# Two halves of P times V summed in PSUM by VectorE, the memory's part added per group of heads, and lead units in other banks, in a kernel of four interleaved blocks

## The chip, the cores and the metric

The kernel runs on one core of a Trainium2 chip. The metric is the time of one execution on the device, in microseconds (us). A core has one engine for matmuls (PE, TensorE) with its queue of weight loads (PEld), and three others: DVE (VectorE), ACT (ScalarE) and POOL (GpSimd). SP (SyncE) issues the transfers (DMA) used here. Each engine works through its own instructions in a fixed order, so an instruction that waits holds up all that stand behind it on that engine. PE writes to PSUM, which has eight banks of 128 partitions by 512 float32; all else lies in SBUF. A name such as L1412 is line 1412 of the kernel's file. In the changed kernel the numbers are 1 to 11 higher: L1412 is L1421 there, L1426 is L1437.

## The reference

The input x is 1 x 2048 x 640, the result has the same shape. Two blocks, A and B, take turns, each with a LayerNorm ahead and the input added behind:

```
x = x + A(layernorm(x));  x = x + B(layernorm(x))      # twice

A: q, k, v = x @ wq, x @ wk, x @ wv     # 32 heads of 20, 4 segments of 512
   for each segment s:
       a_dot = softmax(q k^T * scale + mask) v          # within the segment
       a_mem = (phi(q) M) / (phi(q) z + 1e-6)           # phi(t) = t + 1 if t > 0 else exp(t)
       o     = sigmoid(beta) * a_mem + (1 - sigmoid(beta)) * a_dot
       M, z  = M + phi(k)^T v, z + sum(phi(k))
   return o @ wo
B: z = gelu(x @ w_in)                   # 640 -> 1728
   z1, z2 = z[:864], layernorm(z[864:])
   return (z1 * (w_sp @ z2 + b_sp)) @ w_out
```

The mask takes out the keys that lie *before* the query in a segment, and keeps the query's own and those behind it. M and z are zero in the first segment, so no memory is read there.

## The kernel before

**Number format.** Every large matmul is done with fp16 operands: a number is split into a high half (its fp16 value) and a low half (what is left, again in fp16), and of the four products three are summed. Splits are the bulk of the work beside PE: for the probabilities P, ACT takes the exponential (L1358) and the high half (L1376), POOL the low half (L1377).

**Stages, as they lie in the profiled execution.** Up to 113 us: loads, the scaling of weights, and the lead of the first attention layer. 113 to 612 us: first attention. 612 to 1221 us: first mixer (block B: its first phase ends with `zp`, L334; the second multiplies along the tokens, L713, and goes back with `cyp`, evicted at L749). From 1207, partly inside the mixer's end, to 1254: lead of the second attention layer. 1254 to 1736: second attention. 1736 to 2271: second mixer.

**Attention.** Heads go in pairs; two pairs take NS = 5 steps (so there are two combines in five steps, 64 of each kind in the two layers), and a step t of the program consists, on PE, of

- the scores for the row maxima `mp` of step t + 8 (LM = 8), with keys as columns, and the scores `es` of step t with keys as rows, each with its mask matmuls (L1351, L1322). DVE reduces `mp` to maxima (L1365, L1368), ACT takes exp of `es`;
- every five steps, the transpose of the maxima `mtp` (L1384), which go back as a bias row of the queries by way of the split at L1387 and DMAs (L1390);
- matmuls that fill the time: the projection to queries and keys (`unit`, L1185), to values (L1128) and the output projection (`yps`, L1161), drawn from generators along the string `order` ("02 03 v4 04 v5 ..."); the memory's `update` (L1277) and `read` (L1247) at fixed steps, with `post` for what follows one or more steps later;
- P times V, `pvs` (L1412), of step t - 2 (LV = 2). Its left operands are P's halves, its right ones V of a head as 41 columns: 20 of V's high half, one of ones (the row sum of P), 20 of V's low half. So one matmul gives the product with both halves of V side by side, 41 columns per head and 128 queries, and a pair of heads fills 8 x 41 = 328 columns of one bank.

After the third and the fifth of five steps a pair is complete, and `combine` (L1417) follows: DVE forms 1 / (row sum * gate) in `rs` (L1425, L1426), multiplies all 328 columns by it into the SBUF tile `ab` (L1430), and POOL adds the two halves into `oat` (L1431) and, from the second segment on, the memory's part `gm` (L1433). After the last pair of a group (6 heads, the fifth group 8) the inner function `out` runs two steps later: ACT copies `oat` to fp16 (L1441), POOL subtracts (L1442), SP stores (L1447).

**PE's order** is written out by hand: the attention phases and the mixer's first phase stand under a manual schedule for PE, so PE's rows are in program order. **The order on DVE, ACT, POOL and SP** is set by a scheduler that plays the program through with costs of its own; it may put any instruction ahead of another that it doesn't depend on. A tile of a pool that is laid on addresses of an earlier tile waits for that tile's last reader, wherever the tile was named. So a change of the size of one tile shifts others, and with them what waits for what.

**PSUM.** The pool of tag `dn` has banks 0 and 1 (projections), `mp` 2 and 3, `ms` 4 (transposes, updates, reads), `es` 5 and 6, `pv` 7. There is one buffer for each tag but `dn`, which has two.

**The lead.** Before step 0 there are LEAD = 12 steps, -12 to -1, in which projections of the first segment run before any probability is there; `mp` starts at step -8. The units of head rows (0,0) and (0,1) (segment, row of 128) are done ahead of the lead, and their two memory updates are kept in `self.wait` until the lead; (0,2) and (0,3), v4 and (0,4) come in the lead itself. Each k goes from its bank through `out`: scaled high and low halves, then exp and max for phi, which is written back to the bank, and `keys` reads it from there (L1218, L1219).

**The mixer's first phase** loads x1 rows (L293), makes their statistics and LayerNorm (L235 to L244) and splits (L250, L252), and multiplies (`zp`, L334).

## Time and profile before

| | |
|---|---|
| three runs | 2265.99, 2270.63, 2275.52 us; median 2270.63 us |
| profiled execution | 2273.17 us; span from first to last instruction 2271.4 us |
| granted PE clock, mean over the span | 0.985 |
| PE busy | 2121.0 us, 93% |
| PEld busy (overlaps PE) | 1292.5 us, 57% |
| DVE | 1467.5 us, 65% |
| ACT | 1167.1 us, 51% |
| POOL | 991.0 us, 44% |
| transfers | 349 MB, mean 154 GB/s |

The profile is of one execution. Its rows come in a few forms. A stretch reads `from:to length`, then for PE, PEld, DVE, ACT and POOL the busy time with the count of instructions in brackets, then the granted clock of PE (1.00 is full), the share of time in which the transfer engines were busy, and GB/s. A row of waits reads: who waited, the line, for which instruction of which engine, us in total, how often, the longest. A row of the timeline reads: start, duration, engine, line, operation, destination and sources with shapes, how many of the same were joined in the row, and in brackets how long the engine had stood before it and what ended that. A row of a group reads the same without a start: count, then busy us and mean ns of one, then idle time just before and its releasers. Shares of the span are means over stages of different kinds: POOL's 44% holds the mixer's second phases, in which it does almost nothing.

### The profile page before, as it was taken

To read this page: it belongs to the slowest core of one execution; us is meant where nothing else is said; L and a number is where in the kernel's file an instruction comes from. 1 tells how busy PE (TensorE), PEld (TensorE's weight loads), DVE (VectorE), ACT (ScalarE), POOL (GpSimd) and SP (SyncE) were. 2 spreads that over 40 slices of the span, in tenths; PEclk is the share of its full clock that TensorE was granted. 3 is DMA by queue.
4 is the path that set the end of the run, shared out by engine and by line. 5 is a ranking of instruction groups with operands and counts; after the bars stand their busy time and mean duration, and the time that the engine had idled before them with its cause. 6 is when DMAs were issued, how large, how long until landed. Compare 5 with 4: busy or idle time off the path is not lost. (4 is left out here: it accounts for less than half of the span.)

```text
span 2271.4 us, 49058 instructions
## 1 busy us (share of the span) xinstructions
PE 2121.0 (93%) x19911; PEld 1292.5 (57%) x19911; DVE 1467.5 (65%) x2686; ACT 1167.1 (51%) x1400; POOL 991.0 (44%) x804
## 2 busy tenths in 40 slices
PE   4888898988699999999998898999999999999999
PEld 2455565656455555555554556666665555555655
DVE  8588878686744555545433787786766767455455
ACT  3298888786622332222222797888875334323221
POOL 2198989987610100100001698889985323000000
PEclk9999999998999999999999999999999999999999
DMA  5534634455645669977756345344467334977876
GB/s 163 152 107 112 175 96 128 117 148 138 160 122 153 169 174 230 239 224 190 177 150 153 84 101 149 88 116 109 125 179 182 94 109 104 257 211 190 226 209 135
DMA packets 511428, 349.02 MB, mean 154 GB/s; under 512 B 409889, under 2 KB 447649, under 8 KB 506081
## 3 DMA queue, kind: packets, MB, share of 16 engines
q1 hardware_dynamic: 511200, 345.88, 58.7%
q8 instruction: 156, 2.56, 0.5%
q14 instruction: 72, 0.58, 0.1%
HBM read 156.51 MB, written 101.21 MB: 113 GB/s over the span
## 5 line engine op out<-in xcount | busy, mean ns | idle before, releaser
L1377 POOL TENSOR_TENSOR PHL<-P,PHL 128x1024 f16<-128x1024 f32 x310 | 659.0, 2134 | 155.3 <-ACT PHL L1376 149.1
L1358 ACT ACTIVATE P<-es,sc 128x1024 f32<-128x1024 f32 x320 | 355.9, 1112 | 109.6 <-PE es L1322 101.0
L1368 DVE TENSOR_REDUCE mx<-mp 128x2 f32<-128x1024 f32 (+2 forms) x384 | 319.8, 859 | 51.4 <-PE mp L1322 51.1
L238 POOL TENSOR_TENSOR lnrs<-lnve,mhalf 128x1 f32<-128x1 f32 x92 | 56.4, 621 | 656.5 <-DVE lnve L237 627.7
L1376 ACT CAST PHL<-P 128x1024 f16<-128x1024 f32 x320 | 333.3, 1042 | 5.8
L334 PEld LDWEIGHTS <-th 128*128 128x128 f16 x1920 | 188.2, 98 | 179.0 <-DMA th<-xnhl 16.1
L713 PE MATMUL gp<-zh,wt 128*128 128x432 f16 x1024 | 231.2, 346 | 0.0
L713 PEld LDWEIGHTS <-wt 128*128 128x128 f16 x1536 | 150.2, 98 | 128.9
L1412 PEld LDWEIGHTS <-PHL 128*128 128x128 f16 x5120 | 166.5, 96 | 73.6 <-DVE ab L1430 22.0
L499 PEld LDWEIGHTS <-wt 128*128 128x128 f16 x1344 | 131.3, 98 | 113.4 <-DMA wt<-wn 1.1
L1412 PE MATMUL pv<-vs,PHL 128*128 128x41 f16 x5120 | 174.2, 181 | 22.3 <-DVE ab L1430 14.1
L1128 PE MATMUL vps<-wvh,xt 128*128 128x320 f16 x640 | 155.3, 305 | 15.4 <-DVE vs L1134 12.7
L334 PE MATMUL zp<-wi1h,th 128*128 128x432 f16 x640 | 150.0, 349 | 14.9 <-DMA th<-xnhl 14.6
L1351 PE MATMUL mp<-qk 60*128 60x512 f16 (+3 forms) x1024 | 126.6, 305 | 23.5 <-DVE mx L1368 14.1
L1351 PEld LDWEIGHTS <-qk 60*128 60x128 f16 (+1 forms) x2048 | 78.8, 94 | 116.2 <-issue 94.8
L1351 PE MATMUL es<-qk 64*128 64x256 f16 (+3 forms) x1024 | 124.5, 298 | 17.2 <-ACT P L1358 9.2
L713 PE MATMUL gp<-zl,wt 128*128 128x432 f16 x512 | 135.3, 346 | 0.0
L1185 PE MATMUL kps<-xt,wkh 128*128 128x512 f16 x380 | 124.5, 390 | 8.1 <-DVE phl L1219 8.1
L1185 PE MATMUL qps<-xt,wqh 128*128 128x512 f16 x380 | 122.1, 383 | 0.9 <-DMA xt<-xnhl 0.9
L1161 PE MATMUL yps<-woh,o 128*128 128x320 f16 x480 | 117.9, 305 | 4.6 <-DVE x L1167 2.6
L1128 PEld LDWEIGHTS <-xt 128*128 128x128 f16 x960 | 88.9, 100 | 51.6 <-issue 12.2
L726 DVE TENSOR_TENSOR u<-u,cz 128x864 f32<-128x864 f32 x16 | 16.9, 1059 | 142.4 <-ACT u L724 134.7
(265 smaller groups left out, 4153.2 us busy)
## 6 DMA issues: line engine op xcount, KB each, us to landing
wr<-in_B_w_sp_dram SPq DMA_DIRECT2D x32, 1024.0 KB
qk<-st SPq DMA_DIRECT2D x256, 120.0 KB
x<-x SPq DMA_DIRECT2D x56, 320.0 KB
z<-z SPq DMA_DIRECT2D x32, 432.0 KB
cz<-z SPq DMA_DIRECT2D x32, 432.0 KB
turned<-wt SPq DMA_DIRECT2D x24, 512.0 KB
wt<-turned SPq DMA_DIRECT2D x24, 512.0 KB
st<-qhl SPq DMA_DIRECT2D x40, 256.0 KB
```

Source lines behind the costliest of these rows:

```text
L334: nc.tensor.matmul(zp[:, n, :FHH], a[:, k, :], b[:, k, c:c + FHH], start=(k == 0 and j == 0), stop=(k == KD - 1 and j == 2))
L499: nc.tensor.matmul(o[:, :FHH], wt[:, x, m, :], zb[b][:, y, m, :], start=start and i == j == 0, stop=i == NP - 1 and j == 2, skip_group_che ...
L713: nc.tensor.matmul(gp[:, n, :FHH], ready[t][:, k % 2, a, k // 2, :], b[:, k, n * FHH:(n + 1) * FHH], start=(i == 0 and j == 0), stop=(i == ...
L1128: nc.tensor.matmul(ps, a[:, k, c], b[:, k, n * 320:(n + 1) * 320], start=(i == 0), stop=(i == 14))
L1161: nc.tensor.matmul(ps, a[:, k, :], b[:, k, c], start=(i == 0), stop=(i == 14))
L1185: nc.tensor.matmul(ps, a[:, k, c], b[:, k, :], start=(i == 0), stop=(i == 14))
L1351: nc.tensor.matmul(out[:, h, o:o + w], a[r, ac], b[r, bc], start=o == 0, stop=False, skip_group_check=True)
L1358: self.last_of["ACT"] = nc.scalar.activation(self.Pf[t], es, AF.Exp, scale=g.esc).ins
L1368: self.last_of["DVE"] = nc.vector.tensor_reduce(mx[:, e, :, i], mp[:, :, o:o + w], AX.X, ALU.max).ins
L1376: nc.scalar.copy(hl[:, 0], P)
L1377: (nc.gpsimd if t < self.T - self.TAIL or t % 2 == 0 else nc.vector).tensor_tensor(hl[:, 1], P, hl[:, 0], ALU.subtract)
L1412: nc.tensor.matmul(pv[:, i, h, :], self.P[u][:, x, h, o:o + 128], v[:, j, h0 + h, :], start=first and h == x == 0 and (u, o, i, j) == todo[0],
```

## The change

Four edits stand in the diff, and a fifth follows from one of them.

1. In `pvs` each head and query tile has 42 columns (PVC), of which 41 are written as before; 8 x 42 = 336. In `combine` a DVE `tensor_reduce` adds the halves pairwise, from 8 x 40 columns of the bank to 160 columns of the same bank that are free (336 to 495, `sums`), and a DVE product multiplies these by `rs` straight into `oat`. The product with `ab` on DVE and the add on POOL are gone, and so is `ab`.
2. The memory's part is added once for a group of heads, in `out`, on POOL, ahead of ACT's copy: 30 adds of 480 or 640 columns in place of 96 of 160.
3. In the lead, q and k of unit (0,2) go to the two `es` banks (tile `qk02`), and k of (0,3) to the `pv` bank (`k03`). Both are idle there until step 0.
4. The first update that was kept for the lead goes to step -10 instead of -11; the second stays at -9.
5. `ab` took 1312 bytes of a partition. Without it `phq` and what lies behind it (`xt` of x1 among them) lie 1312 bytes lower. The mixer's first x1 tile, at bytes 164320 to 166880 in both kernels, overlapped `ab` (163808 to 165120); now it overlaps `phq`.

```diff
--- before.py
+++ after.py
@@ -825,6 +825,7 @@
 UH = [range(6 * m, 6 * m + 6) if m < 4 else range(24, 32) for m in range(NU)]
 TH = [range(min(128 * m // DH, UH[m][0]), (128 * m + 127) // DH + 1) for m in range(NU)]
 NS = 5
+PVC = 2 * (DH + 1)
 KCH = ((0, 2), (1, 2)), ((0, 0),), ((0, 1), (0, 3)), ((1, 0),), ((1, 1), (1, 3))
 QCH = ((0, 3),), ((0, 2), (0, 0)), ((1, 3),), ((1, 2), (1, 0)), ((0, 1), (1, 1))
 BIG = 60000.0
@@ -1177,7 +1178,7 @@
         xh, xl = self.xt[s % 2][:, 0], self.xt[s % 2][:, 1]
         for nm in ("q", "k") if own is None else own:
             wh, wl = g.w[nm]
-            ps = self.pd.tile([128, L], F32, tag="dn", name=f"{nm}ps") if own is None else own[nm]
+            ps = self.bank(s, m, nm) if own is None else own[nm]
             c = slice(128 * m, 128 * m + 128)
             i = 0
             for k in range(KD):
@@ -1186,6 +1187,15 @@
                     i += 1
                     yield 216
             self.out(nm, s, m, ps)
+
+    def bank(self, s, m, nm):
+        if (s, m) == (0, 2):
+            if nm == "q":
+                self.idle = self.pe.tile([128, 2, 512], F32, tag="es", name="qk02")
+            return self.idle[:, "qk".index(nm)]
+        if (s, m, nm) == (0, 3, "k"):
+            return self.po.tile([128, 512], F32, tag="pv", name="k03")
+        return self.pd.tile([128, L], F32, tag="dn", name=f"{nm}ps")
 
     def out(self, nm, s, m, ps):
 
@@ -1396,9 +1406,8 @@
         n = 2 * (t // NS) + c // 3
         first = c in (1, 3)
         if first:
-            self.pv[n] = self.po.tile([128, 512], F32, tag="pv", name="pv")[:, :8 * 41].rearrange(
-                "p (h t c) -> p t h c", h=2, t=4)
-        pv = self.pv[n]
+            self.pv[n] = self.po.tile([128, 512], F32, tag="pv", name="pv")
+        pv = self.pv[n][:, :8 * PVC].rearrange("p (h t c) -> p t h c", h=2, t=4)
         v = self.vs[s % 2]
         todo = []
         for u in (t - c, t) if first else (t,):
@@ -1409,7 +1418,7 @@
         for h in range(2):
             for u, o, i, j in todo:
                 for x in range(2):
-                    nc.tensor.matmul(pv[:, i, h, :], self.P[u][:, x, h, o:o + 128], v[:, j, h0 + h, :], start=first and h == x == 0 and (u, o, i, j) == todo[0],
+                    nc.tensor.matmul(pv[:, i, h, 0:PVC - 1], self.P[u][:, x, h, o:o + 128], v[:, j, h0 + h, :], start=first and h == x == 0 and (u, o, i, j) == todo[0],
                                      stop=x == 1 and j == (0, 1, 1, 3)[i], skip_group_check=True)
         del self.P[t]
         if c == 3:
@@ -1417,7 +1426,9 @@
 
     def combine(self, n, s, m, h0):
         g, nc = self.g, self.nc
-        T = self.pv.pop(n)
+        pv = self.pv.pop(n)
+        T = pv[:, :8 * PVC].rearrange("p (h t c) -> p t h c", h=2, t=4)
+        sums = pv[:, 8 * PVC:8 * (PVC + DH)].rearrange("p (h t c) -> p h t c", h=2, t=4)
         if (s, m) not in self.ot:
             self.ot[s, m] = self.pl2.tile([128, 4, 8, DH], F32, tag="ot", name="oat")
         ot = self.ot[s, m]
@@ -1426,11 +1437,9 @@
         nc.vector.reciprocal(rs, rs)
         c = h0 - UH[m][0]
         o = ot[:, :, c:c + 2, :]
-        ab = self.pl1.tile([128, 4, 2, 41], F32, tag="ab", name="ab")
-        nc.vector.tensor_tensor(ab, T, rs.unsqueeze(3).to_broadcast((128, 4, 2, 41)), ALU.mult)
-        nc.gpsimd.tensor_tensor(o, ab[:, :, :, 0:DH], ab[:, :, :, DH + 1:], ALU.add)
-        if s > 0:
-            nc.gpsimd.tensor_tensor(o, o, self.gm[s, m][:, :, c:c + 2, :], ALU.add)
+        both = T.rearrange("p t h (i d) -> p h t d i", i=2)[:, :, :, 0:DH]
+        nc.vector.tensor_reduce(sums, both, AX.X, ALU.add)
+        nc.vector.tensor_tensor(o, sums.rearrange("p h t c -> p t h c"), rs.unsqueeze(3).to_broadcast((128, 4, 2, DH)), ALU.mult)
         if h0 + 2 < UH[m][-1] + 1:
             return
 
@@ -1438,6 +1447,8 @@
             nh = len(UH[m])
             hl = self.e1.tile([128, 2, D], F16, tag="xh", name="ohl")[:, :, :4 * nh * DH].rearrange("p i (t h d) -> p i t h d", t=4, d=DH)
             oh, ol = hl[:, 0], hl[:, 1]
+            if s > 0:
+                nc.gpsimd.tensor_tensor(ot[:, :, :nh, :], ot[:, :, :nh, :], self.gm[s, m][:, :, :nh, :], ALU.add)
             nc.scalar.copy(oh, ot[:, :, :nh, :])
             nc.gpsimd.tensor_tensor(ol, ot[:, :, :nh, :], oh, ALU.subtract)
             c = slice(UH[m][0] * DH, (UH[m][0] + nh) * DH)
@@ -1575,7 +1586,7 @@
                     streams.remove(e)
 
         for i, w in enumerate(self.wait):
-            self.later[2 * i - LEAD + 1] = [lambda w=w: self.update(*w)]
+            self.later[i - LEAD + 2] = [lambda w=w: self.update(*w)]
         self.later.setdefault(-5, []).append(lambda: self.start(True))
         fetches = {}
         for n in range(N):
```

**Order on DVE around one combine** (attention, the pair whose combine starts at 138 us of the trace before; `rs` and its reciprocal open a combine, `mx` are the row maxima of another step, 128x2x2 those of two heads at once). Before:

```order
L1425 TENSOR_TENSOR rs<-pv,iomg 128x8
L1426 RECIPROCAL rs<-rs 128x8
L1430 TENSOR_TENSOR ab<-pv,rs 128x328
L1368 TENSOR_REDUCE mx<-mp 128x2 x2
L1202 SCALAR_TENSOR_TENSOR qhl<-qps,qhl 128x512
L1207 TENSOR_SCALAR qps<-qps,sc 128x512
```

and after the change:

```order
L1436 TENSOR_TENSOR rs<-pv,iomg 128x8
L1437 RECIPROCAL rs<-rs 128x8
L1441 TENSOR_REDUCE pv<-pv 128x160
L1378 TENSOR_REDUCE mx<-mp 128x2 x2
L1442 TENSOR_TENSOR oat<-pv,rs 128x4x40
L1212 SCALAR_TENSOR_TENSOR qhl<-qps,qhl 128x512
L1217 TENSOR_SCALAR qps<-qps,sc 128x512
```

The last reader of the `pv` bank was the third instruction; now it is the product, and the two maxima that stood behind the combine stand ahead of it.

**Order on SP at the end of the first attention layer** (L1169 and L1170 store x1 rows behind the output projection, L293 are the mixer's loads of x1 rows, L130 loads of weights, L1447 and L1458 the stores of o, L252 the transposing transfers that the mixer's first matmuls need). Before:

```order
L1169 DMA x_0_9<-x_10213 128x640
L1143 DMA_TRANSPOSE o<-o_2 128x10x128
L130 DMA wst<-in_B_w_in_dram 128x288
L1152 DMA xt<-in_A_x_dram 128x640
L130 DMA wst<-in_B_w_in_dram 128x288
L1169 DMA x_0_10<-x_10347 128x640
L130 DMA wst<-in_B_w_in_dram 128x288
L1169 DMA x_0_11<-x_10473 128x640
L293 DMA x_10693<-x_0_0 128x640
L293 DMA x_10705<-x_0_1 128x640
L1447 DMA o_3<-ohl 128x4x160 x2
```

and after the change:

```order
L1170 DMA x_0_7<-x_9714 128x640
L1153 DMA xt<-in_A_x_dram 128x640
L293 DMA x_10595<-x_0_0 128x640
L130 DMA wst<-in_B_w_in_dram 128x288 x4
L293 DMA x_10607<-x_0_1 128x640
L1170 DMA x_0_8<-x_9913 128x640
L1153 DMA xt<-in_A_x_dram 128x640
```

The loads of x1 stood behind the store of row 11 of x1; now they stand ahead of that of row 8. The first L252 moved up in the same way, from behind the last store of o to ahead of the store of row 9.

**Order on DVE in the first lead** (`khl` and `phl` are the splits of k and of its feature; `qk_672` is the tile `qk02`, `k_816` the tile `k03`). Before:

```order
L1202 SCALAR_TENSOR_TENSOR khl<-kps,khl 128x512
L1207 TENSOR_SCALAR kps<-kps,sc 128x512
L1368 TENSOR_REDUCE mx<-mp 128x2
L1540 MEMSET wap 128x40
L1209 SCALAR_TENSOR_TENSOR kps<-eq,sc,kps 128x512
L1219 SCALAR_TENSOR_TENSOR phl<-kps,sc,phl 128x512
L1202 SCALAR_TENSOR_TENSOR qhl<-qps,qhl 128x512
```

and after the change:

```order
L1212 SCALAR_TENSOR_TENSOR khl<-qk_672,khl 128x512
L1217 TENSOR_SCALAR qk_672<-qk_672,sc 128x512
L1378 TENSOR_REDUCE mx<-mp 128x2
L1551 MEMSET wap 128x40
L1219 SCALAR_TENSOR_TENSOR qk_672<-eq,sc,qk_672 128x512
L1378 TENSOR_REDUCE mx<-mp 128x2 x2
L1229 SCALAR_TENSOR_TENSOR phl<-qk_672,sc,phl 128x512
L1212 SCALAR_TENSOR_TENSOR qhl<-qps,qhl 128x512
```

The rows are the same ones on other banks; the last reader of k (`phl`) stands two maxima later.

## The prediction

> **What bounds the kernel now.** I read the stretches by engine first, then the waits of each attention phase, then the timeline at the phases' borders. These are the two attention phases and a stretch of the mixer (columns: busy time and count by engine, granted clock, DMA share, GB/s):
>
> ```profile
> 113.00:602.00 489.00, 437.26 (x6227) 292.19 (x6221) 392.54 (x739) 403.98 (x490) 427.01 (x316) 0.98 0.52 130
> 1254.00:1734.00 480.00, 447.09 (x6391) 298.49 (x6390) 364.09 (x672) 394.87 (x467) 414.27 (x301) 0.99 0.48 122
> ...
> 1900.00:2000.00 100.00, 100.00 (x571) 55.66 (x569) 56.55 (x81) 34.53 (x39) 12.43 (x13) 1.00 0.77 202
> ```
>
> The mixer leaves PE no idle time; nothing in the change can help there. In the attention phases PE idles 489 - 437.3 = 51.7 us and 480 - 447.1 = 32.9 us, while POOL is busy 87 and 86%, ACT 83 and 82%, DVE 80 and 76%. So a steady-state gain has at most 85 us to come from, and a loss has three other nearly full engines to show itself on. Who waits, in the first phase and then in the second (us in total, times, longest):
>
> ```profile
> ACT P L1358 <- PE es L1322: 53.3, 57, 5.3
> PE mp L1351 <- DVE mx L1368: 9.3, 16, 3.2
> PE pv L1412 <- DVE ab L1430: 9.3, 12, 1.8
> PE es L1351 <- ACT P L1358: 6.3, 9, 1.8
> PE pv L1412 <- POOL PHL L1377: 3.9, 6, 1.6
> ```
>
> ```profile
> PE pv L1412 <- DVE ab L1430: 4.8, 6, 1.8
> PE pv L1412 <- POOL PHL L1377: 3.4, 5, 1.5
> ACT P L1358 <- POOL oat L1433: 1.9, 3, 1.1
> ```
>
> ACT waits for PE, and through ACT so does POOL. PE is the leader, held up by DVE more than by POOL. A stall of PE is therefore mostly paid, and POOL's relief is worth little beyond what PE and ACT wait for it.
>
> **First part: where the mixer's x1 tile lies (a gain).** After the first attention phase PE stands still:
>
> ```profile
> 611.70 0.33 SPq L1169 DMA_DIRECT2D x<-x  x1
> 612.67 0.47 POOL L1431 TENSOR_TENSOR oat<-ab 128x160 f32<-128x160 f32 x1 [2.97 <-DVE ab L1430]
> 613.16 0.80 SPq L293 DMA_DIRECT2D x<-x  x2
> 624.55 0.90 PE L334 MATMUL zp<-wi1h,th 128*128 128x432 f16 x2 [13.15 <-DMA th<-xnhl]
> 615.80:629.50 13.70, 4.95 (x14) 2.11 (x15) 5.11 (x12) 1.45 (x2) 1.40 (x3) 0.50 0.77 185
> ```
>
> SP issues the mixer's first loads (L293) 0.02 us after POOL has read `ab` for the last time (612.67 + 0.47): x1 and `ab` share addresses. With `ab` gone, x1 lies on `phq`, whose last reader runs earlier, and the order of SP shows both loads many rows earlier. The wait of 13.15 us goes, and with it the half clock after it: PE's 4.95 us there at clock 0.50 would be 2.5 us shorter. Together -15.6 us. What is late next? The second phase already loads x1 early, and pays:
>
> ```profile
> 1707.22 1.29 DVE L235 BATCH_NORM_STATS2 lnst<-x 128x6 f32<-128x320 f32 x3 [2.48 <-DMA x<-x]
> 1710.62 0.28 PE L1384 MATMUL mtp<-ident,mx 128*16 128x128 f32 x1 [2.12 <-DVE mx L1365]
> 1713.80 0.61 PE L1351 MATMUL es<-qk 64*128 64x512 f16 x2 [1.21 <-ACT P L1358]
> 1711.50:1718.30 6.80, 5.59 (x50) 3.07 (x50) 5.48 (x9) 5.48 (x7) 5.81 (x5) 0.50 0.51 140
> ```
>
> DVE stands in its queue before the statistics of x1 until the load lands; the maxima behind them (mx L1365) come late, so PE waits 2.12 us, then 1.21 us more, and runs 6.8 us at half clock: 2.1 + 1.2 + 3.4 = 6.7 us. The first phase's new order has the same neighbours, so this may come there too: 0 to 6.7, of which I take half, 3.3. First part: -12.3 us (-9 to -15.6).
>
> **Second part: lead units in other banks, the first update later (a gain).** PE's waits in the two leads, the DVE instruction that ends a third, and clocks behind them:
>
> ```profile
> 86.81 1.01 PE L1185 MATMUL kps<-xt,wkh 128*128 128x512 f16 x2 [2.28 <-DVE phl L1219]
> 99.34 0.30 PE L1128 MATMUL vps<-wvh,xt 128*128 128x320 f16 x1 [3.04 <-DVE vs L1134]
> 1239.28 0.59 PE L1185 MATMUL kps<-xt,wkh 128*128 128x512 f16 x2 [2.27 <-DVE phl L1219]
> PE vps L1128 <- DVE vs L1134: 2.3, 1, 2.3
> 1224.55 0.88 DVE L749 SCALAR_TENSOR_TENSOR xo<-cyp,xs,cx 128x640 f32<-128x640 f32 x1 [5.47 <-DMA x<-xo]
> 86.75:90.16 3.41, 3.35 (x14) 1.08 (x14) 1.81 (x4) 0.60 (x1) 0.00 (x0) 0.50 0.42 99
> 100.40:103.80 3.40, 3.40 (x14) 1.76 (x12) 1.40 (x2) 0.20 (x1) 0.00 (x0) 0.50 1.01 146
> 1240.40:1243.90 3.50, 3.50 (x14) 1.04 (x8) 1.29 (x2) 0.00 (x0) 0.00 (x0) 0.51 0.60 150
> ```
>
> All four waits are for one of the two `dn` banks, held until `keys` has read it for the last time (L1219), or behind such a unit. With (0,2) and the k of (0,3) elsewhere nothing in the order holds these four up: -(2.28 + 3.04) and -(2.27 + 2.3). Each of the three half-clock stretches costs 1.7 us and would go with the wait ahead of it: -5.1. In the second lead the new bank isn't idle: `es` is banks 5 and 6, and the mixer's last `cyp` lies in 4 and 5 until DVE's L749 ends at 1224.55 + 0.88 = 1225.43. PE now runs three matmuls of q of unit (0,2) first and then waits there with the first update, whose bank 4 is held as long; after the change it waits with the unit itself, so those three come later: +0.65 (3 x 216 ns, from the generator's own pace; the row of 1239.28 has 0.59 for two overlapped). The update's new place thus gains nothing: its wait is only handed on. Second part: -8.7 and -5.6, -14.3 us; 0 at worst, if waits come back one unit later, behind which PE has 04 and the value units queued.
>
> The Trainium skill (TensorE: Matmul & The Clock Gate, "What's actually happening") puts the half clock after about 3.4 us of idle, so the waits of 2.3 and 3.0 us would not cause it, and by that rule the part is 9.2. The rows show half clock within 2 us behind three waits that short, so they stay in.
>
> **Third part: the pv bank is held longer (a loss).** Prices from the groups of one shape:
>
> ```profile
> L1368 DVE TENSOR_REDUCE mx<-mp 128x2 f32<-128x1024 f32 x128 | 155.6, 1216 | 30.0 <-PE mp L1322 29.8
> L1430 DVE TENSOR_TENSOR ab<-pv,rs 128x328 f32<-128x328 f32 x128 | 63.5, 496 | 9.4 <-POOL oat L1431 0.5 <-DVE rs L1426 0.5
> L1368 DVE TENSOR_REDUCE mx<-mp 128x2 f32<-128x256 f32 x128 | 52.9, 413 | 0.0
> ...
> L1283 DVE TENSOR_TENSOR mst<-mup,bmask 128x168 f32<-128x168 f32 (+1 forms) x30 | 9.5, 318 | 13.9 <-PE mup L1279 13.4
> ```
>
> The new reduce reads 320 elements: (1216 - 413) / 768 = 1.05 ns each, so 413 + 64 x 1.05 = 480 ns; if its 160 outputs cost as inputs do, 650. The new product of 160 from PSUM is nearest to L1283, 0.31 us. Against 0.50 for `ab`, DVE gets +0.3 us (to +0.46) in each of 128 combines, 38 us in all, on an engine with 20% to spare. What matters is where it stands: `ab` freed the bank at once, and now the scheduler puts the maxima of the step between the reduce and the product that frees the bank. A case (DVE, then PE):
>
> ```profile
> 138.38 0.16 DVE L1425 TENSOR_TENSOR rs<-pv,iomg 128x8 f32<-128x8 f32 x1
> ...
> 138.89 0.50 DVE L1430 TENSOR_TENSOR ab<-pv,rs 128x328 f32<-128x328 f32 x1
> 139.30 1.28 DVE L1368 TENSOR_REDUCE mx<-mp 128x2 f32<-128x768 f32 x2
> ```
>
> ```profile
> 139.46 1.04 PE L1412 MATMUL pv<-vs,PHL 128*128 128x41 f16 x24
> 140.64 0.39 PE L1351 MATMUL mp<-qk 60*128 60x256 f16 x4
> ```
>
> `ab` ends at 139.39, pv starts at 139.46. After the change the product ends at 139.30 + 1.28 + 0.31 = 140.9: pv 1.5 us later. Behind it stand the next scores, es for ACT with them. But these waited for the maxima until 140.6 anyway; pv takes about 0.6 when its inputs are there, so they start at 141.5, 0.9 us later than 140.64. After the second combine of five steps a whole step follows (pv rows 3 us behind `ab`), and nothing is due.
>
> Of the 64 first combines, the order has two maxima newly inside in 27, one in 14, none in 23: up to 1.5, 1.2 and 0.3 us longer. Less the time that lay between the end of `ab` and the next pv (first combines from 125.8 to 1731.7; under 0.1 us in 22, median 0.7) that sums to 36 us; less PE's own idle time in the 6 us behind each, 23. I take +23 (0 if POOL and ACT set the pace, 36 if nothing is absorbed). The Trainium skill (VectorE: DVE Perf Modes, "Rules for kernel authors") speaks against the change: it calls tensor_reduce the slowest DVE operation, to be kept off a hot path. The rows above give the same rate per element for it as for `ab`; what hurts here is its place.
>
> **Fourth part: POOL's relief (a gain).**
>
> ```profile
> L1431 POOL TENSOR_TENSOR oat<-ab 128x160 f32<-128x160 f32 x128 | 65.1, 508 | 20.8 <-DVE ab L1430 19.6 <-ACT PHL L1376 1.0 <-PE es L1322 0.2
> L1433 POOL TENSOR_TENSOR oat<-oat,gm 128x160 f32<-128x160 f32 x96 | 52.7, 549 | 5.4
> L1442 POOL TENSOR_TENSOR ohl<-oat,ohl 128x480 f16<-128x480 f32 x32 | 35.6, 1114 | 3.4 <-ACT ohl L1441 2.7 <-PE pv L1412 0.7
> ```
>
> POOL loses 65.1 + 52.7 us and 20.8 us of standing before `ab`; it gets 30 group adds, nearest to L1442, 1.1 us each (24 of 480 columns, 6 of 640): 35 us. Net -83 us of work. Paid out are only the waits for POOL quoted above: 3.9 + 3.4 by pv and 1.9 by ACT: -9 us (0 to -12). Each group add now stands ahead of ACT's copy of the group, behind which ACT's next exponential is queued: +1 us in all, since ACT has 17% to spare (30 x 1.1 = 33 at worst, if it never had).
>
> **The sum.** -12.3 - 14.3 + 23 - 9 + 1 = -11.6 us. The profiled execution took 2273.2 (span 2271.4 and 1.8 around it); the median of the runs is 2270.6, 2.6 lower. -11.6 from the median: **2259 us**.
>
> **Rivals.** (a) *The pv wait decides*: all 36 us are paid, and the lead's waits come back in part (-9): -12.3 - 9 + 36 - 1 + 1 = +15, 2286, slower. It speaks for it that 22 of the 64 have no slack and that PE leads; against it, that other waits of PE (9.3 us for the maxima alone) shrink when it comes late. It decides from 34 us of paid stall on. (b) *POOL set the pace after all*: its 87% is the highest share beside PE's; then the pv stalls fall where PE would wait anyway (+8), and POOL pays 12: -12.3 - 14.3 + 8 - 12 + 1 = -30, 2241. Against it: POOL waits for ACT, ACT for PE. (c) *Gains at the borders don't arrive*: the first phase's early x1 costs what the second's does (-9), the lead's waits move one unit on (-4): -9 - 4 + 23 - 9 + 1 = +2, 2273. The change does what it says, except that the later first update is idle.
>
> **Chances.** Forecast 0.40 (its own range 2252 to 2266), (a) 0.22, (b) 0.25, (c) 0.13. About 0.5%, 11.4 us, is what a measurement of this kernel can tell from no change. The forecast lies on that bound, half of it on either side (0.20, 0.20); (b) is faster; (c) is same 0.10 and slower 0.03; (a) is slower 0.18, same 0.04. With 0.01 rounded over: faster 0.45, same 0.34, slower 0.21. The range 2236 to 2285 takes in (b) and (c) and most of (a).
>
> **What would show it.** Right: the first zp of the first layer follows the last pv within 3 us, without half clock; no wait of `kps` or `vps` for DVE in the leads; PE's wait of pv for DVE grows from 14 us to 35 or more, with the product as its releaser; POOL's share falls under 80%. Wrong: pv's wait stays under 20 us (then b), or PE's idle time in the attention phases grows by more than 30 us (then a), or idle time of 5 us or more stands before the first zp (then c).

## The result

The changed kernel takes 2283.35 us (median of 7 runs, 2280.24 to 2287.17), the kernel before in the same comparison 2274.24 (7 runs). The ratio, taken over all these runs and not from the two medians, is 1.0052, with a 95% interval from 1.0032 to 1.0072: slower by 12 us, between 7 and 16. The forecast was 11.6 us faster.

The page of the changed kernel opens with

```profile
span 2285.2 us, 48909 instructions
PE 2127.4 (93%) x19911; PEld 1294.7 (57%) x19911; DVE 1479.5 (65%) x2814; ACT 1169.5 (51%) x1400; POOL 923.7 (40%) x610
```

POOL works 67 us less, DVE 12 us more, and the span is 13.8 us longer. To see where, I cut both traces at the same events: the start of the first exponential P of a layer, the end of its last pv, the start of the first and the end of the last zp. Lengths of the stages in us (differences of starts and ends of those instructions, one profiled execution each; the last stage ends with PE's last matmul, some 3.5 us ahead of the end of the span; kernels of the experiments stand here too, to be read later):

| kernel | to first P | attention 1 | to first zp | zp phase 1 | last zp to first P of layer 2 | attention 2 | to the end |
|---|---|---|---|---|---|---|---|
| before | 113.9 | 497.5 | 13.1 | 194.4 | 445.2 | 471.5 | 532.3 |
| after | 114.9 | 509.6 | 0.2 | 191.9 | 446.9 | 486.1 | 532.1 |
| combine_undone | 112.5 | 496.5 | 0.3 | 191.8 | 446.8 | 476.9 | 531.4 |
| product_first | 116.8 | 493.1 | 0.4 | 191.7 | 447.0 | 470.7 | 531.7 |
| ab_last | 117.0 | 507.4 | 0.3 | 192.0 | 447.4 | 485.7 | 531.0 |
| pf_old_lead | 112.2 | 495.5 | 0.2 | 191.9 | 442.9 | 468.1 | 532.0 |
| pf_late_update | 107.4 | 498.1 | 0.3 | 191.9 | 441.9 | 470.1 | 531.8 |

Each row is one execution, and the 23 runs of the kernel before that were timed beside ab_last lie between 2261.03 and 2277.48 us; so a single cell carries no verdict, a pattern over rows does. Before to after: the two attention phases grow by 12.1 and 14.6 us, the border of the first layer loses 12.9 and the zp phase behind it 2.4 more, and the two leads, which should have lost 14.3, grow by 1.0 and 1.7.

PE's largest waits in the two attention phases of the changed kernel (same cuts; us in total, times, longest; `...` stands for rows left out):

```profile
PE pv L1421 <- DVE oat L1442: 24.0, 21, 2.2
PE es L1361 <- ACT P L1368: 10.6, 12, 1.9
PE mp L1361 <- DVE mx L1378: 8.1, 9, 3.4
```

```profile
PE pv L1421 <- DVE oat L1442: 15.6, 18, 2.0
...
PE pv L1421 <- POOL PHL L1387: 3.4, 3, 2.5
...
PE mp L1361 <- DVE mx L1378: 3.0, 7, 0.8
```

The wait of pv for DVE was 9.3 and 4.8 us; it is 24.0 and 15.6, and the instruction that ends it is the product L1442. The increase is 25.5 us. The phases grew by nearly as much, 26.7, but not by these waits alone, as their stretches show (the first phase before and after, then the second):

```profile
113.89:611.40 497.51, 444.43 (x6334) 297.57 (x6332) 399.54 (x752) 409.79 (x498) 433.75 (x321) 0.98 0.51 130
114.89:624.46 509.57, 449.50 (x6334) 299.64 (x6333) 410.04 (x827) 412.14 (x500) 402.54 (x227) 0.97 0.51 130
1264.08:1735.60 471.52, 438.61 (x6334) 294.70 (x6333) 358.99 (x665) 392.51 (x463) 414.98 (x302) 0.99 0.48 123
1263.52:1749.63 486.11, 442.69 (x6334) 295.24 (x6333) 365.44 (x728) 393.94 (x463) 378.97 (x206) 0.98 0.47 119
```

PE's idle time (length less busy time) grew by 7.0 and 10.5 us, 17.5 in all: other waits became shorter, those for the maxima among them. The other 9.1 us are the same 6334 matmuls of each phase taking longer, at a granted clock that is lower by 0.01 in each.

The place that the prediction took as its case shows how the wait comes about (timeline of the changed kernel):

```profile
139.08 0.16 DVE L1436 TENSOR_TENSOR rs<-pv,iomg 128x8 f32<-128x8 f32 x1
139.27 0.20 DVE L1437 RECIPROCAL rs<-rs 128x8 f32<-128x8 f32 x1
139.39 0.45 DVE L1441 TENSOR_REDUCE pv<-pv 128x160 f32<-128x320 f32 x1
139.75 1.28 DVE L1378 TENSOR_REDUCE mx<-mp 128x2 f32<-128x768 f32 x2
140.94 0.31 DVE L1442 TENSOR_TENSOR oat<-pv,rs 128x160 f32<-128x160 f32 x1
141.31 0.79 PE L1421 MATMUL pv<-vs,PHL 128*128 128x41 f16 x24 [1.00 <-DVE oat L1442]
```

Of the 2.2 us from the start of `rs` to pv, the maxima take 1.28, and pv stands for 1.00.

In the first lead the two waits for a `dn` bank are gone, and another stands there (DVE, SP and PE, and the stretch behind it):

```profile
88.95 0.74 DVE L1229 SCALAR_TENSOR_TENSOR phl<-qk,sc,phl 128x512 f16<-128x512 f32 x1
89.76 1.23 SPq L1231 DMA_TRANSPOSE pk<-phl  x1
93.69 0.25 PE L1287 MATMUL mup<-vs,pk 128*128 128x168 f16 x1 [4.49 <-DMA pk<-phl]
94.00:98.00 4.00, 4.00 (x21) 2.20 (x18) 0.35 (x2) 1.17 (x2) 0.00 (x0) 0.57 0.00 0
```

The same transfer and the same update in the kernel before:

```profile
87.95 1.24 SPq L1221 DMA_TRANSPOSE pk<-phl  x1
91.74 0.25 PE L1277 MATMUL mup<-vs,pk 128*128 128x168 f16 x1
```

The update is that of unit (0,2), at a fixed step of PE, and its operand `pk` is the transposed feature of that unit's k. In the kernel before PE came to it 10.9 us after the end of that k, and `pk` was there. Now PE comes to it after 7.0 us, earlier by 3.9 us: the wait of 2.28 us is gone, and so is the half clock behind it. `phl`, ready to run when ACT's half of it ended at 87.34, stands in DVE's order behind two maxima and a reduction of a weight and ends at 89.69; the transfer lands at 93.7. PE waits 4.49 us and then runs at a clock of 0.57 over 4 us. In the second lead (changed kernel, and in the last row the first wait of this lead in the kernel before):

```profile
1222.62 1.01 PE L1186 MATMUL qk<-xt,wqh 128*128 128x512 f16 x2 [5.08 <-DVE xo L749]
1244.12 0.25 PE L1287 MATMUL mup<-vs,pk 128*128 128x168 f16 x1 [2.96 <-DMA pk<-phl]
1245.00:1250.00 5.00, 5.00 (x31) 2.76 (x29) 1.79 (x4) 1.17 (x2) 0.00 (x0) 0.69 0.07 26
...
1225.48 0.23 PE L1277 MATMUL mup<-vs,pk 128*128 128x147 f16 x1 [3.49 <-DMA qk<-st]
```

The first wait is longer by 1.6 us than the 3.49 of the kernel before, and the clock is 0.50 for 6.7 us (1220.8 to 1227.5) where it was for 3.4 (1226.8 to 1230.2). The prediction had put +0.65 us on this place.

The border of the first layer did what was forecast:

```profile
587.09 0.55 SPq L293 DMA_DIRECT2D x<-x  x1
623.89 0.57 PE L1421 MATMUL pv<-vs,PHL 128*128 128x41 f16 x16
624.69 0.53 PE L334 MATMUL zp<-wi1h,th 128*128 128x432 f16 x2 [0.23 <-DVE x L1168]
```

x1 is loaded 26 us earlier, and PE stands idle for 0.23 us before the first zp in place of 13.15.

So the theory after the result (A): the place of the product costs some 23 us, the border brings some 13, the new lead brings nothing since the update's wait takes its gain, and POOL's relief brings nothing. Its rivals: the new combine costs by its length or DVE's load, not its place; the early x1 costs in the attention phase what it brings at the border; the lead's gain is there and lost elsewhere.

### The profile page after: what moved, and what is told of

Read it like the earlier page. It is cut to its first block, busy times and chain, and to the rows that moved or that the text cites. A ratio compares the mean times of both kernels' runs of the same rounds, so it can differ in the third digit from the quotient of the medians.

```text
span 2285.2 us, 48909 instructions
## 1 busy us (share of the span) xinstructions
PE 2127.4 (93%) x19911; PEld 1294.7 (57%) x19911; DVE 1479.5 (65%) x2814; ACT 1169.5 (51%) x1400; POOL 923.7 (40%) x610
## 5 line engine op out<-in xcount | busy, mean ns | idle before, releaser
L1378 DVE TENSOR_REDUCE mx<-mp 128x2 f32<-128x1024 f32 (+2 forms) x384 | 321.4, 860 | 43.3 <-PE mp L1332 40.6
L238 POOL TENSOR_TENSOR lnrs<-lnve,mhalf 128x1 f32<-128x1 f32 x92 | 57.7, 634 | 642.3 <-DVE lnve L237 612.5
L1186 PE MATMUL qps<-xt,wqh 128*128 128x512 f16 x360 | 115.3, 382 | 0.0
L1186 PE MATMUL kps<-xt,wkh 128*128 128x512 f16 x340 | 110.4, 385 | 3.4 <-DVE phl L1229 3.4
```

The source lines that it names most:

```text
L1186: nc.tensor.matmul(ps, a[:, k, c], b[:, k, :], start=(i == 0), stop=(i == 14))
L1378: self.last_of["DVE"] = nc.vector.tensor_reduce(mx[:, e, :, i], mp[:, :, o:o + w], AX.X, ALU.max).ins
```

## The experiments

Ratios are to the kernel before, timed on the same chip, with 95% intervals. Where two experiments are compared, the difference is that of their ratios, in us of some 2271, and it is uncertain by some 6 us.

### The combine

**all_but_combine**: the changed kernel with the old combine. So that x1 stays early, `ab` gets a pool of its own behind that of xt1.

```diff
-        self.e1, self.e2, self.bg, self.pl1, self.u4, ax = ...
+        self.e1, self.e2, self.bg, self.pl1, self.u4, ax, self.pab = ...
...
+        ab = self.pab.tile([128, 4, 2, 41], F32, tag="ab", name="ab")
+        nc.vector.tensor_tensor(ab, T, rs.unsqueeze(3).to_broadcast((128, 4, 2, 41)), ALU.mult)
+        nc.gpsimd.tensor_tensor(o, ab[:, :, :, 0:DH], ab[:, :, :, DH + 1:], ALU.add)
```

> The changed kernel with the combine as it was (product of 328 columns into ab on DVE, add of the halves on POOL); ab stands in a pool of its own at addresses that the mixer's x1 doesn't touch, so the early x1, the group add and the lead units in other banks all stay. Theory A (the wait of pv for the product costs the attention phases some 26 us, and nothing else in the change costs much): 24 to 28 us below the changed kernel, 2255 to 2260; pv waits for DVE 14 us or less over both phases; P0 to the last pv takes 496 to 500 us in the first layer and 470 to 474 in the second. Theory B (the early x1 and its statistics lengthen the first attention phase, the new lead the second): the time stays within 8 us of the changed kernel, above 2272, and both phases keep more than half of their extra 12 and 14.6 us.

Measured: 2271.44 us, ratio 1.0002 [0.9988, 1.0016]. That is 0.5% below the changed kernel, half of what A says, and outside both forecasts. The phases did shrink, to 499.3 and 469.7 us; the loss is in the zp phase, 202.9 us against 191.9 (PE's waits from 612 us on):

```profile
PE zp L334 <- ACT wi0h L90: 4.3, 4, 2.1
PE zp L334 <- DVE wi0l L91: 1.2, 2, 1.0
```

The pool that I gave to `ab` lies under the mixer's weight tile wi0, whose split now came late. So this run holds a second change, and the next one is without it.

**combine_undone**: the same with that pool below all tiles of the mixer that are needed early.

```diff
-        self.e1, self.e2, self.bg, self.pl1, self.u4, ax = ...
+        self.pab, self.e1, self.e2, self.bg, self.pl1, self.u4, ax = ...
...
-            pool("bp", 1).tile([128, 480], F32, name="bp")
+            pool("bp", 1).tile([128, 544], F32, name="bp")
```

> Again the changed kernel with the old combine (ab, POOL's add of the halves), but with ab in a pool below the mixer's tiles: in all_but_combine it lay under the weight tile wi0h, and the mixer's first zp waited 5.5 us for wi0h and wi0l, with half clock behind, so that its first phase took 8 us more than in the changed kernel. Theory A (the new combine, as scheduled, costs some 25 us in the two attention phases): 2258 to 2264, 20 to 26 us below the changed kernel; no wait of zp for wi0h. Theory B (POOL's relief in the new combine was worth something, so undoing it loses that too): 2266 or above.

Measured: 2261.51 us, ratio 0.9949 [0.9928, 0.997]. No wait for wi0; 1.03% or 23 us below the changed kernel. A holds: the change without its new combine is a gain of 12 us.

**product_first**: the changed kernel, with the maxima of each step held behind the product of the last combine.

```diff
+        self.product = nc.vector.tensor_tensor(o, sums..., rs..., ALU.mult).ins
...
+                with tc.issue_after(self.product):
                     self.last_of["DVE"] = nc.vector.tensor_reduce(mx[...], mp[...], AX.X, ALU.max).ins
```

> The changed kernel, with each step's maxima (mx) held in DVE's order behind the product of the combine before them. The same instructions; nothing stands between reduce and product in 45 of the 64 first combines (7 before). Theory A1 (it is the place of the product, behind maxima of 0.4 to 1.2 us each): the wait of pv for DVE falls from 39.6 us to some 20 us, the time by 12 to 18 us to 2265 to 2271. Theory A2 (it is the length of the new combine itself, 0.3 us more, and DVE's load): pv's wait stays above 30 us and the time above 2278. What A1 may lose again: maxima that come later, seen as waits of mp for mx, 8 us so far.

Measured: 2259.68 us, ratio 0.9951 [0.9934, 0.9967], 23 us below the changed kernel: A1, with more than it forecast. Nowhere does a maximum stand between `rs` and the product (in the changed kernel in 53 of 64 first and 49 of 64 second combines). PE's waits, over the whole execution:

```profile
PE mp L1361 <- DVE mx L1380: 25.5, 53, 2.6
PE pv L1423 <- DVE oat L1444: 13.8, 17, 2.8
...
PE pv L1423 <- POOL PHL L1389: 2.4, 5, 1.5
```

and the groups of DVE that belong to the combine:

```profile
L1443 DVE TENSOR_REDUCE pv<-pv 128x160 f32<-128x320 f32 x128 | 57.4, 448 | 0.0
L1444 DVE TENSOR_TENSOR oat<-pv,rs 128x160 f32<-128x160 f32 x128 | 41.2, 322 | 4.0
```

The same instructions, of the same length, on the same engine: pv waits 13.8 us, as in the kernel before (14.1). What A1 might lose again was lost too: the maxima come later, and mp's wait for them (both lines) went from 15.7 us in the changed kernel to 31.9. The time fell even so. Compared with combine_undone (0.9949) the new combine, once its product stands ahead of the maxima, shows neither gain nor loss: 0.45 + 0.32 against 0.50 us on DVE, 128 times, and POOL's 65 us less, come to no difference that can be measured.

**ab_last**: the counterpart. The *old* combine of combine_undone, its product `ab` held behind the step's maxima.

```diff
+        self.product = lambda: self.close(n, s, m, h0, ab, T, rs, o, ot)
+    def close(self, n, s, m, h0, ab, T, rs, o, ot):
+        with self.tc.issue_after(self.last_of["DVE"]):
+            nc.vector.tensor_tensor(ab, T, rs..., ALU.mult)
+        nc.gpsimd.tensor_tensor(o, ab[:, :, :, 0:DH], ab[:, :, :, DH + 1:], ALU.add)
...
             self.scores(t)
+            self.product()
```

> combine_undone with the same old combine, but its product ab held in DVE's order behind the maxima of the step, as the changed kernel has its product: two maxima stand between rs and ab in 60 of the 64 first combines and one in 58 of the second ones (11 and 12 so far). No instruction is added or lengthened. Theory A1 (the place of the instruction that frees the pv bank is the whole loss): pv's wait for DVE rises from some 13 to 35 us or more, the time to 2285 or above (24 us or more over combine_undone). Theory A2 (the loss needs the longer new combine too): 10 us or less over combine_undone, below 2272.

Measured: 2283.66 us, ratio 1.0053 [1.0034, 1.0071]: 1.04% or 23.6 us above combine_undone. PE's waits:

```profile
PE pv L1421 <- DVE ab L1444: 38.9, 43, 2.2
PE mp L1360 <- DVE mx L1377: 12.0, 14, 2.9
```

The same wait (39.6 in the changed kernel) and the same loss, without one longer instruction. The place of the product among the maxima on DVE is enough for the whole loss; POOL's add, which reads `ab`, moves back with it.

**reduce_to_sbuf**: the changed kernel, with the reduce writing into `oat` and the product in place there, so that the bank is free after the reduce.

```diff
-        nc.vector.tensor_reduce(sums, both, AX.X, ALU.add)
-        nc.vector.tensor_tensor(o, sums.rearrange("p h t c -> p t h c"), rs..., ALU.mult)
+        nc.vector.tensor_reduce(o.rearrange("p t h d -> p h t d"), both, AX.X, ALU.add)
+        nc.vector.tensor_tensor(o, o, rs..., ALU.mult)
```

> The changed kernel, but the reduce writes straight into oat in SBUF and the product works there in place, so the pv bank is free after rs and the reduce (about 0.16 + 0.48 us), earlier than in the kernel before (rs, reciprocal, ab: about 0.8). Same count of instructions, same POOL. Theory A (the time for which the bank is held decides): pv's wait for DVE is below the 14 us of the kernel before, the attention phases are not longer than before, the time is 2250 to 2260. Theory B (DVE's added work decides, wherever it stands): the time stays above 2272.

Measured: 2296.21 us, ratio 1.0118 [1.0099, 1.0137], the slowest of all. A's first half held: pv waits only 1.5 us for the reduce, over the whole execution. But mp waits 28.6 and 22.4 us for the maxima (lines L1378 in the two phases; 8.1 and 3.0 in the changed kernel), and DVE got much busier:

```profile
L1442 DVE TENSOR_TENSOR oat<-oat,rs 128x160 f32<-128x160 f32 x128 | 123.2, 962 | 1.8
L1441 DVE TENSOR_REDUCE oat<-pv 128x160 f32<-128x320 f32 x128 | 61.3, 479 | 0.0
```

A product of the same size took 0.32 us when it read PSUM, and takes 0.96 here. It takes either about 0.3 or up to 2.27, and this is one of the long ones:

```profile
1652.63 2.13 POOL L1387 TENSOR_TENSOR PHL<-P,PHL 128x1024 f16<-128x1024 f32 x1 [0.56 <-ACT PHL L1386]
1652.67 2.27 DVE L1442 TENSOR_TENSOR oat<-oat,rs 128x160 f32<-128x160 f32 x1
1654.86 1.21 DVE L1378 TENSOR_REDUCE mx<-mp 128x2 f32<-128x1024 f32 x1
```

POOL's subtraction starts 0.04 us earlier and runs 2.13; the product, which reads two SBUF operands, ends 0.18 us behind it. Of the 128 products, 93 began while an instruction of POOL was running (those of L238, 128x1, left aside), and each of them ended 0.18 to 0.26 us behind that instruction. The other 35, 9 of which began just ahead of a POOL instruction, took 0.30 to 0.33 us. The Trainium skill (SBUF — State Buffer, "Who interferes with whom") says that a DVE instruction with two inputs in SBUF contends with a GpSimd instruction that reads SBUF, that the ports which the two engines share are an exclusive lock, and that the order of issue decides who blocks; the trace agrees. The product of the changed kernel reads only `rs` from SBUF and is spared: 92 of its 128 began inside one of POOL's subtractions, and none took longer than 0.33 us. So this run says nothing against the theory of the place, but the longer products hid what an earlier free bank would have brought, and that remains open.

### The border of the first layer

**x1_early**: the kernel before with the move of `ab` of all_but_combine, alone.

> The kernel before, with ab moved out of the pool that the mixer's x1 lies on, and nothing else: the loads of x1 go up in SP's order to ahead of the store of row 8. Theory A (that alone takes the 13 us of idle time ahead of the first zp): -11 to -14 us, ratio 0.994 to 0.995; the first zp within 1 us of the last pv; the first attention phase (P0 to last pv) is at most 2 us longer. Theory B (the early statistics of x1 block DVE): the phase is 5 us or more longer and the time falls by 8 us or less.

Measured: 2266.91 us, ratio 0.9977 [0.9966, 0.9988], outside A and by its size with B; but B's mechanism isn't there, the first attention phase took 495.4 us, 2.1 less than before. The zp phase took 202.8, with the same waits for wi0:

```profile
PE zp L334 <- ACT wi0h L90: 4.2, 3, 2.1
PE zp L334 <- DVE wi0l L91: 1.4, 2, 1.2
```

**x1_early_2**: the same with the pool of combine_undone.

> The kernel before with ab in that same pool below the mixer's tiles and nothing else; x1 then touches only mr (its loads stand behind the store of row 8 of x1), wi0h is untouched. Theory A (the early x1 alone takes the 13 us ahead of the first zp, and the early statistics cost nothing, as the first attention phase of x1_early took 2 us less than before): -10 to -14 us, ratio 0.994 to 0.9955. Theory B (part of the 13 us comes back): -6 us or less.

Measured: 2259.64 us, ratio 0.9947 [0.9927, 0.9967]: 12 us faster, as A has it. So the place of one tile of 1312 bytes is worth half of what the place of the product costs. What the early statistics of x1 cost, the traces leave open: the first attention phase was 502.9 us here and 495.4 in x1_early, against 497.5.

### The lead

**pf_old_lead**: product_first with the lead of the kernel before.

```diff
-            ps = self.bank(s, m, nm) if own is None else own[nm]
+            ps = self.pd.tile([128, L], F32, tag="dn", name=f"{nm}ps") if own is None else own[nm]
...
-            self.later[i - LEAD + 2] = [lambda w=w: self.update(*w)]
+            self.later[2 * i - LEAD + 1] = [lambda w=w: self.update(*w)]
```

> product_first with the lead as in the kernel before: all q and k in the two dn banks, the first update at step -11. Theory A (the new lead only hands the wait on to the update of unit (0,2), which waits 4.5 us for the transposed pk, and costs 1 to 3 us in the first layer and 2 to 4 in the second): 3 to 7 us below product_first, 2252 to 2257 (ratio 0.992 to 0.9935). Theory B (the new lead gains what was predicted, hidden by other moves): 2262 or above.

Measured: 2253.6 us, ratio 0.9916 [0.9897, 0.9936], 0.35% or 8 us below product_first. In the table its first P comes 4.6 us earlier, its second lead is 4.1 us shorter. So the new lead isn't only no gain; beside this combine it costs (A, with slightly more than the 3 to 7 us that it forecast). The waits that it removes are back here (PE, 78 to 118 us):

```profile
PE vps L1129 <- DVE vs L1135: 3.0, 1, 3.0
PE kps L1186 <- DVE phl L1229: 2.3, 1, 2.3
```

**pf_late_update**: product_first with the new lead, the updates that follow k in the lead five steps behind it, not three.

```diff
-                self.post(3, lambda: self.update(s, m, pk), True)
+                self.post(3 if self.now >= 0 else 5, lambda: self.update(s, m, pk), True)
```

> product_first with the updates of (0,2), (0,3) and (0,4) that follow their keys in the lead posted 5 steps behind them in place of 3. Theory A (the update of (0,2) waits for the chain of k to phl to pk because it stands too early): its wait of 4.5 us in the first lead goes, P0 comes 3 to 5 us earlier, likewise in the second layer; time 4 to 8 us below product_first, 2252 to 2256. Theory B (what ends last ahead of step 0 is elsewhere: the maxima or the q and k of (0,3)): P0 stays within 1 us, the time within 2 us of product_first.

Measured: 2244.61 us, ratio 0.9876 [0.9855, 0.9896]: 17 us below product_first, twice what A forecast, and 28 us faster than the kernel before (by the ratio). Of PE's waits between 78 and 118 us

```profile
PE mp L1361 <- DVE mx L1376: 1.8, 2, 1.1
PE mup L1287 <- DMA pk<-phl: 1.4, 1, 1.4
```

are the largest that are left. The first P comes at 107.4 in place of 116.8 us, the second lead is 5.1 us shorter. But product_first holds the loss that the early update brings. What the forecast priced is the new lead against the old one, and that comparison is with pf_old_lead: 0.40% or 9 us, some 3 to 15. So the new lead does gain once the update gives its operand time. What the later update would bring in the old lead, no run shows.

**late_update_only**: that edit alone on the changed kernel.

> The changed kernel with the lead's updates posted 5 steps behind their keys in place of 3, and nothing else. Theory A (the lead's gain was there, and was taken up by the update's wait for pk; it is independent of the combine): 12 to 17 us below the changed kernel as in pf_late_update against product_first, 2266 to 2271; P0 of the first layer at 106 to 109 us (114.9). Theory B (it is only a gain where DVE serves the maxima as in product_first): 6 us or less.

Measured: 2272.63 us, ratio 0.9999 [0.9982, 1.0016]: 0.53% or 12 us below the changed kernel, at the low end of A's 12 to 17; the time itself is just above its 2266 to 2271. The first P comes at 111.0 us, 3.9 earlier rather than the 6 to 9 of the forecast; the second lead is 4.6 us shorter. So the later update gains beside the late product too. Against the kernel before, with the old lead, the two leads are shorter by 2.9 us each.

**q02_in_pv**: pf_late_update with q of (0,2) in the pv bank and k of (0,2) and (0,3) in the `es` banks.

```diff
             if nm == "q":
-                self.idle = self.pe.tile([128, 2, 512], F32, tag="es", name="qk02")
-            return self.idle[:, "qk".index(nm)]
+                return self.po.tile([128, 512], F32, tag="pv", name="q02")
+            self.idle = self.pe.tile([128, 2, 512], F32, tag="es", name="k0203")
+            return self.idle[:, 0]
         if (s, m, nm) == (0, 3, "k"):
-            return self.po.tile([128, 512], F32, tag="pv", name="k03")
+            return self.idle[:, 1]
```

> pf_late_update, but q of (0,2) goes to the pv bank, and k of (0,2) and k of (0,3) to the two es banks. In the second lead the unit waited 5.2 us for the mixer's last eviction, which holds the lower es bank; now the 15 matmuls of q (3.2 us) can run in that time. If theory A (the wait is only for that bank) holds: the wait of 5.2 falls to some 2 us, with less half clock behind it, and the time by 2 to 4 us, 2240 to 2243. Theory B (the update's bank, held as long, or q's own input sets the start): within 1 us of pf_late_update, the wait handed on.

Measured: 2244.61 us, ratio 0.9889 [0.987, 0.9909], not to be told from pf_late_update, as B has it. Waits in the second lead, of the matmuls of k and of the update:

```profile
PE k L1186 <- DVE phl L1230: 2.3, 1, 2.3
PE mup L1288 <- DMA pk<-phl: 2.2, 1, 2.2
PE k L1186 <- DVE xo L749: 1.9, 1, 1.9
```

The wait for the mixer's eviction fell from 5.2 to 1.9 us as A says, and a wait of 2.3 us for `phl` came in each lead: again a wait handed on. The second lead is 2.5 us shorter than in pf_late_update (439.4 us), and the first P comes 2.1 us later (109.5).

### POOL

**group_gm**: the kernel before with only the memory's part added per group.

```diff
-        if s > 0:
-            nc.gpsimd.tensor_tensor(o, o, self.gm[s, m][:, :, c:c + 2, :], ALU.add)
...
+            if s > 0:
+                nc.gpsimd.tensor_tensor(ot[:, :, :nh, :], ot[:, :, :nh, :], self.gm[s, m][:, :, :nh, :], ALU.add)
             nc.scalar.copy(oh, ot[:, :, :nh, :])
```

> The kernel before with the memory's part added per group: POOL loses 96 adds of 0.55 us and gets 30 of 1.2 to 1.6 us. Theory A (POOL's load isn't what the attention phases wait for): within 0.2% of the kernel before. Theory B (POOL's relief pays, as the prediction's fourth part had it): 4 us or more below it. Theory C (the group add ahead of ACT's copy costs): 4 us or more above it.

Measured: 2274.54 us, ratio 1.0017 [1.0002, 1.0031]: 4 us slower (0.5 to 7): inside A's 0.2%, at the edge of C and against B. Less work on POOL brought nothing. If the 4 us are real, the add ahead of ACT's copy may be what costs, but this run doesn't show it: the waits of pv for POOL's PHL were 8.1 us here, 7.3 in the kernel before.

## Why the prediction was wrong

Its sum, beside what the runs give for the same terms (us of some 2271, from the ratios above):

| term | predicted | measured | from |
|---|---|---|---|
| border, layer 1 | -12.3 | -12 (-17 to -7) | x1_early_2 against before |
| pv bank held longer | +23 | +23 and +23.6 | after against product_first; ab_last against combine_undone |
| lead | -14.3 | +2.7; +8 | leads of after against before; product_first against pf_old_lead |
| POOL's relief and the group add | -9 + 1 | +4 for the adds of `gm`; 0 for the rest of it | group_gm against before; product_first against combine_undone |
| sum | -11.6 | +12 | after |

The terms of single runs add up to 18 to 23, more than the 12 measured, and each is uncertain by some 3 to 6 us. A sum with fewer steps closes: combine_undone (all but the combine) is 12 us faster than before, and the place of the product costs 24, as ab_last shows, which makes +12.

**First part, right.** The mechanism, the place and the size held: x1 lay on `ab`, 13 us of idle time and the half clock behind it went. Whether the early statistics block DVE, as half of the 6.7 us, wasn't settled. One thing wasn't seen: where `ab` goes matters as well. In x1_early it lay under wi0, and 7 of the 12 us were lost again.

**Second part, wrong, and the step that decides.** "With (0,2) and the k of (0,3) elsewhere nothing in the order holds these four up": true of the four instructions, and their waits went. But the units were not the only work with a fixed place. The update of (0,2) stands three steps behind its k, and its chain (exp, feature on DVE, split, transposing transfer) takes its time: 11.5 us now, from the end of k on PE at 82.2 until 93.7. PE had arrived late enough in the kernel before, because of the very waits that were removed. The lower bound named, "waits come back one unit later", was what happened, and it should have been the value: in the trace before, the transfer of `pk` is issued at 87.95 and PE uses it at 91.74 without a wait, and in the second layer PE waits 2.24 us for the same kind of transfer and starts 4.4 us after its issue; so there was hardly any slack, and what came off ahead of the update would come back at it. The order listing showed `phl` two maxima later on top. The second lead's first wait and the half clock behind it were sized too low as well (+0.65 us; the wait grew by 1.6 us, and the half clock lasted 3.3 us longer). With the update two steps later the lead gains, but less than 14.3: 9 us (3 to 15) by pf_late_update against pf_old_lead, and 5.8 by the two leads of late_update_only against before. As to the half clock, the trace after shows a clock of 0.69 over 5 us behind a wait of 2.96 us (1244.12). The rule weighed there (the Trainium skill, TensorE: Matmul & The Clock Gate, "What's actually happening") asks for about 3.4 us of idle, so the rows were again the better guide.

**Third part, right in mechanism, and in size partly by luck.** The reduce took 448 ns (480 estimated), the product 315 (310). The added length is 34 us on DVE and cost nothing that could be measured; the maxima between cost 23. Pricing the instructions alone would have found only the first. But the 23 of the working are stalls of PE alone, and PE's idle time in the two phases grew by only 17.5 us; the matmuls at a lower clock added 9.1, and for those this part had no term, although the first two parts had one. That the product is the releaser and that pv's wait grows to 35 us or more came as forecast (39.6).

**Fourth part, wrong.** The waits for POOL were counted as paid time, 9 us. They are not. The waits of pv for POOL did shrink, from 7.3 us to 3.9 in the changed kernel and 2.4 in product_first, but neither group_gm nor the comparison of product_first with combine_undone shows any gain. That PE finds its next wait at another engine is likely, and not shown by a run of its own.

**The rivals.** The time lies near where rival (a) put it, +15, but not for its reasons: it had all 36 us of pv's stall paid and 9 us of the lead kept. Its sign, PE's idle time in the attention phases up by more than 30 us, didn't come (17.5), and its own 2286 us lie just outside the range that was to take in most of it. The loss comes from the forecast's own third part, with rival (c)'s idea (the lead's waits move on) and none of POOL's gain. The four signs named as right all came (first zp 0.23 us behind; no wait of kps or vps for DVE in the leads; pv's wait at 39.6; POOL at 79 and 78% of the two phases), and the time was still wrong: two of them ask only whether a wait went, one only for POOL's work, and none asked what PE would wait for next.

## What to carry to other kernels

When an instruction that frees a buffer is split in two, look in the engine's order at what now stands between the parts, before adding up how long they are; holding the second part ahead of its neighbours was worth 23 us here, and the lengthening itself cost nothing that could be measured. When a wait is taken away from the engine that leads, walk on along its fixed order and ask of each operand when it will be there, since waits that were removed may have been what hid the next one. And undo one part at a time, but read the whole stage table of each such run: a moved tile can put a new wait under a quite different tile.

The version that came out best, the changed kernel with the product held ahead of the maxima and the lead's updates two steps later, takes 2244.61 us, 0.9876 [0.9855, 0.9896] of the kernel before.

## What the runs showed of the hardware

A DVE product of 160 columns took 0.32 us with one operand in PSUM and one in SBUF, also when it began inside a POOL subtraction. With both operands in SBUF it took 0.96 us on average and up to 2.27: when it began while POOL was running an instruction larger than 128x1, it ended 0.18 to 0.26 us behind that instruction. The reduce beside it, with its one input in PSUM, stayed between 0.47 and 0.48 us. On a DVE that is about 80% busy this made the kernel in which pv waits least for DVE (1.5 us) the slowest of the study (2296.21 us). A second point, smaller: the granted clock was 0.50 from 94.4 to 97.7 us behind a wait of 4.49 us, and from 1244.7 to 1248.0 behind one of 2.96 us, as it had been behind those of 2.3 and 3.0 us in the kernel before. A lower clock is part of what waits cost here: in the two attention phases the granted clock fell from 0.98 and 0.99 to 0.97 and 0.98, and the same matmuls took 9.1 us longer.
